# A windowed attention beside an S4 convolution: one stacked layout for Q and K, four loads an item, denominators turned on VectorE, wo prepared in steps, a new order of the attention's pieces

## The chip, the cores and the metric

One core of a Trainium2 chip runs the whole program. The metric is the device time in microseconds of one execution.

## The reference, cut to what is computed

```python
def _A_ref(x, wqkv, wo):            # x (1, 2048, 576), 32 heads of 18
    B, S, D = x.shape
    H = 32; Dh = D // H; W = 256
    qkv = (x @ wqkv).reshape(B, S, 3, H, Dh).transpose(2, 0, 3, 1, 4)
    q, k, v = qkv[0], qkv[1], qkv[2]
    scores = jnp.einsum("bhqd,bhkd->bhqk", q, k) * (Dh ** -0.5)
    mask = (idx[:, None] - idx[None, :] >= 0) & (idx[:, None] - idx[None, :] < W)
    p = softmax(jnp.where(mask[None, None], scores, -1e9), axis=-1)
    o = jnp.einsum("bhqk,bhkd->bhqd", p, v)
    return o.transpose(0, 2, 1, 3).reshape(B, S, D) @ wo

def _B_ref(u, A_re, A_im, B_re, B_im, C_re, C_im, log_dt, Dskip):   # u (1, 2048, 576), 128 states
    dt = jnp.exp(log_dt)[:, None]
    P = jnp.exp((dt * A)[:, :, None] * l[None, None, :])
    K = jnp.einsum("dn,dnl,dn->dl", Cc, P, dt * Bc).real
    y = causal_convolution(u, K)    # by FFTs of 4096 points
    return y + u * Dskip[None, None, :]

return jnp.concatenate([a, b], axis=-1)
```

## The kernel before

The program has three stages. In the first, `proj` multiplies x by wqkv (each f32 operand split in two f16 parts, 14 matmuls a tile, `mm14`), beside `tables`, which computes the S4 kernel K from outer products and sines, and `s1_u`, the first step of the convolution's transform of u. A planner gives their instructions an order on each engine. For each of four chunks of 512 rows, `proj` makes nine tiles of 128 channels of Q and K, each as a high and a low f16 part in st (pool pst, two buffers), and SP stores them: Q in qq (part, chunk, channel, row), K in kk (with the last 256 rows of the chunk before in front) and, for chunk 0, in k0. V goes to vd with a column of ones behind each head's 18 columns. The second stage, `s1_k`, is the first transform of the S4 kernel, stored in gk.

In the third stage the order is written out by hand (`manual_schedule`): each engine, and SP's queue with it, runs its instructions as the program issues them. There are 16 items: four chunks of 512 queries times four groups of eight heads. An item has five steps. In each step the loop in `build` advances generators: `att` (two tiles of scores with their exponentials, then the product with V of the step before, into po), `smax` (16 tiles of scores an item, each reduced by DVE to a row maximum, running 20 steps ahead; the maxima go as row 54 into Q, so that the next scores have them subtracted), `conv` (the convolution's spectra, products and inverse, then the last transform from hp), `norm` of the items before, and `wo` (the output projection). All tiles of scores, spectra and projections go through one PSUM ring of three slots (`slot`).

`load(i + 2)` stands in the second step of item i and fills one of three sets: f16 scores take stacked rows, for Q low, high, high and for K high, low, high of the 18 channels of a head (54 rows of each half of 64). It makes nine DMAs: for each half of Q one of 18 rows and one of 36 rows, the latter read twice over,

```python
nc.sync.dma_start(dv[64 * h + 18:64 * h + 54], src[0:1].to_broadcast([2, 18, 4 * n]))
```

for each half of K one of 36 and one of 18 rows, and V. Rows 54 up to 64 of K hold -32768, set by six memsets of POOL.

`norm` divides by the sums of the exponentials, which are rows 18, 50, 82 and 114 of osb (po copied by ACT). Four DMAs bring them to den (128 x 32), DVE takes the reciprocal, one DMA writes it to rd in DRAM, four read it back over 32 partitions each (rb), POOL multiplies, ACT and POOL split the result into two f16 parts, and four DMAs store it in od. `wo` loads od again for a finished chunk (oh, ol) and multiplies.

`wo_load` prepares wo once, at the end of item 0: four times load a quarter, take its absolute value on ACT and its maximum on DVE; then a power of two as scale; then four times load it again and split it in woh and wol. Its tile "raw" has one buffer.

Of the kernel before, what the change touches and what calls it, by code (L numbers as in the profile page):

```python
# [21 lines left out]
CQ = 512  # L22
CK = 768
# [80 lines left out]
class Kernel:  # L104
# [51 lines left out]
    def proj(self):  # L156
        nc, a, wp, dp, sp = self.nc, self.a, self.p["wq"], self.p["dram"], self.p["const"]
        self.qq = dp.tile([2, 4, D, CQ], F16, name="qq")
        self.kk = dp.tile([2, 4, D, CK], F16, name="kk")
        self.k0 = dp.tile([2, D, CQ], F16, name="k0")  # L160
# [33 lines left out]
        for c in range(4):  # L194
# [13 lines left out]
            for m in range(9):  # L208
                ps = self.p["pps"].tile([128, 512], F32, name="pp")
                self.mm14(ps, (wh, wl), (xh, xl), slice(m * 128, m * 128 + 128), slice(0, 512))  # L210
                st = self.p["pst"].tile([128, 2, 512], F16, name="qst")
                nc.scalar.activation(st[:, 0], ps, AF.Copy, scale=S)
                nc.vector.scalar_tensor_tensor(st[:, 1], ps, S, st[:, 0], op0=OP.mult, op1=OP.subtract)
                for z, off, f0 in ((self.qq, 0, 0), (self.kk, 256, D)):
                    r0, r1 = max(m * 128, f0), min(m * 128 + 128, f0 + D)
                    if r0 < r1:
                        s = st[r0 - m * 128:r1 - m * 128]
                        t = z[:, c, :, off:] if c or not off else self.k0
                        nc.sync.dma_start(t[:, r0 - f0:r1 - f0].rearrange("a p c -> p a c"), s)
                        if off and c < 3:  # L220
                            nc.sync.dma_start(z[:, c + 1, r0 - f0:r1 - f0, 0:256].rearrange("a p c -> p a c"),
                                              s[:, :, 256:])
                yield
# [254 lines left out]

    def slot(self):
# [43 lines left out]
    def inverse(self, t, ch, Y):  # L523
# [14 lines left out]
        if ch == 2:  # L538
            v = self.h.rearrange("(t s b c) a l j -> t s c (a l) b j", t=8, s=2, b=2)
            for s in range(2):  # L540
                for c in range(2):
                    nc.sync.dma_start(v[t, s, c ^ s], self.ho[64 * c:64 * c + 64, s])  # L542

    def conv(self):
# [20 lines left out]
        def load(m):  # L565
            hp[m] = fs.tile([128, 2, D], F32, name="hp")
            nc.sync.dma_start(hp[m].rearrange("p l j -> p (l j)"), hv[:, 2 * m * D:2 * m * D + 2 * D])

        load(0)
        for m in range(16):  # L570
            if m < 15:
                load(m + 1)
# [7 lines left out]
            for c in range(2):  # L580
                nc.sync.dma_start(ov[m, c][:, D:], y[64 * c:64 * c + 64].rearrange("p h j -> p (h j)"))
            yield

    def att_setup(self):
# [8 lines left out]
        for b in range(3):  # L593
            d = {"Q": ap.tile([128, 4, CQ], F16, name="Q%d" % b), "K": ap.tile([128, 4, CK], F16, name="K%d" % b)}
            for h in range(2):
                nc.gpsimd.memset(d["K"][64 * h + 32:64 * h + 64], -32768.0)
# [3 lines left out]
    def load(self, i):  # L600
        nc, (c, o), d = self.nc, divmod(i, 4), self.sets[i % 3]
        V = self.p["v"].tile([128, 12 * 76 + 16], F32, name="V")
        for nm, z, seq in (("Q", self.qq, (1, 0, 0)), ("K", self.kk, (0, 1, 0))):
            n = CQ if nm == "Q" or c == 0 else CK
            if n == CQ and nm == "K":
                z = self.k0
                d["k"], d["kc"] = d["K"].rearrange("p t n -> p (t n)")[:, :4 * CQ].rearrange("p (t n) -> p t n", t=4), 256
            elif nm == "K":
                d["k"], d["kc"] = d["K"], 0
            dv = d[nm].rearrange("p t n -> p (t n)")[:, :4 * n]  # L610
            for h in range(2):
                src = z[:, c, 144 * o + 72 * h:144 * o + 72 * h + 72] if z is not self.k0 else z[:, 144 * o + 72 * h:144 * o + 72 * h + 72]
                src = src.rearrange("a (i p) n -> a i (p n)", p=4)
                if nm == "Q":
                    nc.sync.dma_start(dv[64 * h:64 * h + 18], src[1])
                    nc.sync.dma_start(dv[64 * h + 18:64 * h + 54], src[0:1].to_broadcast([2, 18, 4 * n]))
                else:
                    nc.sync.dma_start(dv[64 * h:64 * h + 36], src)  # L618
                    nc.sync.dma_start(dv[64 * h + 36:64 * h + 54], src[0])
        nc.gpsimd.memset(V[:, 912:], 0.0)  # L620
        kc = d["kc"]
        t0 = 8 * c - 4 + kc // 64
        nc.sync.dma_start(V[:, kc // 64 * 76:912], self.vd[o, :, :, t0:8 * c + 8].rearrange("r k t e -> (r k) (t e)"))
        d["V"] = V

    def smax(self, i):
# [3 lines left out]
        for qb in range(8):  # L630
# [4 lines left out]
            for pp in range(2):  # L635
                ps = self.slot()
                for b in range(2):
                    for r in range(2):
# [3 lines left out]
                                         d["k"][rr, 2 * b + pp, k0 - d["kc"]:k1 - d["kc"]], start=True, stop=False, skip_group_check=True)  # L642
# [19 lines left out]
        for b in range(2):  # L662
            src = m16[16 * b:16 * b + 16].rearrange("s (h x) -> h s x", h=2)
            for r in range(2):
                nc.sync.dma_start(q[r:r + 1, 1024 * b:1024 * b + 1024].rearrange("o (s x) -> o s x", x=64), src[r ^ b])
# [30 lines left out]
    def att(self, i):  # L696
        nc, (c, o), d = self.nc, divmod(i, 4), self.sets[i % 3]
        po = self.p["po"].tile([128, 2, 512], F32, name="po")
        first = set()

        def pv(P, bl):
            for rel, o, q0, w in bl:
                kb = rel + 4
                for p in range(4):
                    for z in range(2):
                        nc.tensor.matmul(po[32 * p:32 * p + 32, z, q0:q0 + w],  # L706
                                         d["V"][64 * z:64 * z + 64, kb * 76 + 19 * p:kb * 76 + 19 * p + 32],
# [245 lines left out]
```

## Time and profile before

| | us |
|---|---|
| median of three runs (1357.79 to 1373.87) | 1358.03 |
| the profiled execution | 1366.19 |
| its span, from the first to the last instruction | 1364.4 |

| engine | busy in the span | share | instructions |
|---|---|---|---|
| PE | 844.7 us | 62% | 16426 |
| VectorE (DVE) | 554.0 us | 41% | 780 |
| ScalarE (ACT) | 573.4 us | 42% | 797 |
| GpSimd (POOL) | 287.8 us | 21% | 184 |

The mean granted clock of TensorE is 0.807 of full speed. The queue of SP carries 149.56 MB of the 155.96 MB that are moved. The shares are means over three stages; what bounds each is read from the windows and the waits below. In the rows, "A <- B" after a wait names what the engine waited for, as far as the profile shows it, and SPq is SP's queue of DMA issues.

### The profile page before, as it was taken

What the parts mean: (1) busy time and instruction counts of PE and PEld (TensorE: products, weight loads), DVE (VectorE), ACT (ScalarE), POOL (GpSimd) and SP (SyncE); (2) the same over time, 40 slices, a digit from 0 to 9 for tenths busy, and PEclk for the clock granted to TensorE, in tenths of its full rate; (3) what the DMA queues carried; (4) which work ended last, traced back from release to release, by engine and by line L of the source; (5) the groups of instructions that cost most, each with busy time, mean ns of one, the idle gap of its engine ahead of it and who ended that gap; (6) DMA issues with size and microseconds to landing.
All of it is one profiled execution on the core that took longest, in us unless ns stands there. A gap on an engine that the chain in (4) does not pass through costs nothing. (4 is left out here: it accounts for less than half of the span.)

```text
span 1364.4 us, 36796 instructions
## 1 busy us (share of the span) xinstructions
PE 844.7 (62%) x16426; PEld 500.2 (37%) x16426; DVE 554.0 (41%) x780; ACT 573.4 (42%) x797; POOL 287.8 (21%) x184
## 2 busy tenths in 40 slices
PE   1518898798888955703645465774467565267734
PEld 0204464464455543402322233442244343134413
DVE  3687667856565113413423332342333343132200
ACT  1857887577783221313321332432233243123521
POOL 0033443444342040100211121121021021011110
PEclk9999999988888965757866877976778887578977
DMA  9451242132222363522424343342525232354442
GB/s 271 143 175 64 81 105 88 53 76 90 68 78 67 112 215 148 189 69 67 139 63 117 126 116 120 87 139 77 163 79 175 73 102 61 106 173 135 132 146 87
DMA packets 108223, 155.96 MB, mean 114 GB/s; under 512 B 33745, under 2 KB 71697, under 8 KB 107873
## 3 DMA queue, kind: packets, MB, share of 16 engines
q1 hardware_dynamic: 106528, 149.56, 36.2%
q10 hardware_dynamic: 1504, 3.99, 1.1%
q8 instruction: 129, 2.11, 0.7%
q14 instruction: 30, 0.24, 0.1%
q0 software_dynamic: 32, 0.07, 0.0%
HBM read 94.26 MB, written 58.92 MB: 112 GB/s over the span
## 5 line engine op out<-in xcount | busy, mean ns | idle before, releaser
L654 DVE TENSOR_REDUCE m<-ring 128x2 f32<-128x640 f32 (+4 forms) x256 | 194.1, 780 | 407.2 <-PE ring L649 377.1
L641 PE MATMUL ring<-K,Q 54*64 54x320 f16 (+4 forms) x1024 | 94.1, 350 | 255.3 <-DMA K<-kk 132.7
L739 ACT ACTIVATE P<-ring,esc 128x1024 f32<-128x1024 f32 (+2 forms) x160 | 160.7, 1058 | 88.3 <-PE ring L735 88.3
L364 POOL TENSOR_TENSOR m<-A,tr 128x1024 f32<-128x1024 f32 x72 | 149.5, 2096 | 197.6 <-PE kp L402 165.2
L641 PEld LDWEIGHTS <-Q 54*64 54x64 f16 x1024 | 46.3, 117 | 302.2 <-issue 297.7
L519 POOL TENSOR_TENSOR Y<-t,t 128x384 f32<-128x384 f32 x24 | 24.0, 998 | 500.2 <-DVE t L517 430.2
L512 ACT ACTIVATE X<-ring 128x768 f32<-128x768 f32 x24 | 19.4, 810 | 220.2 <-PE ring L506 220.2
L402 PE MATMUL kp<-Q,m 128*32 128x64 f32 x4608 | 87.9, 229 | 30.3 <-DVE xp L137 10.8
L706 PE MATMUL po<-P,V 64*32 64x320 f32 (+4 forms) x2816 | 101.2, 409 | 0.6 <-issue 0.3
L402 PEld LDWEIGHTS kp<-Q,m 128*32 128x32 f32 x4608 | 74.8, 115 | 59.3 <-issue 36.8
L450 PE MATMUL pp<-ut,wu 64*128 64x288 f32 x128 | 48.0, 602 | 44.1 <-DMA ut<-in_u_dram 18.7
L726 PE MATMUL ring<-Q,K 55*64 55x320 f16 (+4 forms) x1408 | 68.8, 293 | 7.7 <-ACT P L739 2.6
L765 POOL TENSOR_TENSOR osb<-osb,rb 128x1024 f32<-128x1024 f32 x16 | 37.7, 2355 | 140.3 <-DMA Q<-m 84.5
L649 PE MATMUL ring<-sm,idb 64*64 64x128 bf16 x896 | 62.1, 244 | 0.0
L706 PEld LDWEIGHTS po<-P,V 64*32 64x32 f32 x2816 | 45.5, 123 | 39.2 <-issue 30.0
L154 PE MATMUL ring<-woh,oh 128*128 128x288 f16 x160 | 32.3, 334 | 41.9 <-DMA oh<-od 41.0
L154 PEld LDWEIGHTS <-oh 128*128 128x128 f16 x320 | 32.7, 111 | 65.4 <-DMA oh<-od 44.6
L576 PE MATMUL ring<-hp,i 128*64 128x288 f32 x128 | 24.8, 518 | 45.5 <-DMA hp<-h 43.5
L154 PE MATMUL pp<-xh,wh 128*128 128x512 f16 x180 | 48.6, 393 | 2.3 <-DVE xh L205 1.9
L536 ACT ACTIVATE ho<-ring 128x768 f32<-128x768 f32 x24 | 19.4, 810 | 72.5 <-PE ring L533 62.6
L154 PE MATMUL pp<-xh,wl 128*128 128x512 f16 x180 | 48.0, 391 | 0.0
L154 PEld LDWEIGHTS <-wh 128*128 128x128 f16 x324 | 31.5, 100 | 43.3 <-issue 11.0
(146 smaller groups left out, 1607.3 us busy)
## 6 DMA issues: line engine op xcount, KB each, us to landing
gx<-g SPq DMA_DIRECT2D x32, 288.0 KB
gk<-g SPq DMA_DIRECT2D x16, 576.0 KB
tx<-gx SPq DMA_DIRECT2D x8, 1152.0 KB
tk<-gk SPq DMA_DIRECT2D x8, 1152.0 KB
h<-ho SPq DMA_DIRECT2D x32, 288.0 KB
hp<-h SPq DMA_DIRECT2D x16, 576.0 KB
raw<-in_xT_dram SPq DMA_DIRECT2D x16, 512.0 KB
rb<-rd SPq DMA_DIRECT2D x64, 128.0 KB
```

Of the source, the lines that this page charges most:

```text
L154: self.nc.tensor.matmul(ps, u, v, start=(i == 0), stop=(i == len(ops) - 1))
L364: self.nc.gpsimd.tensor_tensor(m, A[:, ch, a0:a0 + 8].unsqueeze(3).to_broadcast(sh), tr[:, ch, part, 0:8].unsqueeze(2).to_broadcast(sh), o ...
L402: nc.tensor.matmul(kp[32 * st:32 * st + 32, c % 2 * JJ2 + j, :], m[:, ch, a0:a0 + 32], Q[:, ch, term % 2, :], start=(term == 0), stop=(ter ...
L450: nc.tensor.matmul(ps[r], self.wu[64 * r:64 * r + 64], ut[64 * r:64 * r + 64, 288 * k:288 * k + 288], start=True, stop=True)
L576: nc.tensor.matmul(ps[64 * c:64 * c + 64, hf, :288], self.i2, hp[m][:, c, 288 * hf:288 * hf + 288], start=True, stop=True, skip_group_chec ...
L641: nc.tensor.matmul(ps[z:z + 64, b, :n], d["Q"][rr, 2 * b + pp, 64 * qb:64 * qb + 64], d["k"][rr, 2 * b + pp, k0 - d["kc"]:k1 - d["kc"]], s ...
L649: nc.tensor.matmul(out, self.idb[rr], self.sm[rr], start=False, stop=True, skip_group_check=True)
L654: nc.vector.tensor_reduce(mv[:, :, 8 * pp + qb], ps[:, :, :n], axis=AX.X, op=OP.max)
L706: nc.tensor.matmul(po[32 * p:32 * p + 32, z, q0:q0 + w], d["V"][64 * z:64 * z + 64, kb * 76 + 19 * p:kb * 76 + 19 * p + 32], P[p % 2][64 * ...
L726: nc.tensor.matmul(ps[z:z + 64, b, off:off + w], d["k"][rr, 2 * b + pp, kc:kc + 64], d["Q"][rr, 2 * b + pp, q0:q0 + w], start=(k == 0), st ...
L739: nc.scalar.activation(P[pp][:, :, lo:hi], ps[:, :, lo:hi], AF.Exp, scale=self.esc)
L765: nc.gpsimd.tensor_tensor(osb, osb, rb, op=OP.mult)
```

## The change

1. Layout: Q and K are stored as the scores read them, qz and kz (chunk, half, 64 rows, 4 heads, 512 columns): the high part twice, the low part once, and rows 54 to 63 filled with -32768 from a tile of ones. A tile of st now takes two stores for each piece of a group of 72 channels.
2. `load` makes four DMAs of 128 rows (three for chunk 0): Q, K, the last 256 columns of K of the chunk before, V. V becomes part of the set.
3. `norm`: DVE transposes osb in blocks of 32 x 32, takes the reciprocal of column 18 of each block and transposes it, broadcast, back. The stores in od move one step later.
4. `wo_load` becomes a generator, advanced once a step from the start; "raw" has two buffers and is loaded two steps ahead; the maximum takes absolute values itself.
5. The order of a step: `att` runs across items and gives its pieces singly (a tile of scores, half of the product with V), with a tile of the maxima after every first or third piece; so the last product of an item falls in the next item's first step.
6. SP's issues of h, y, ya and the row of maxima are put off by `defer` to the next `flush` or the one after, at the start of a step. The last transform loads hp two tiles ahead (three buffers), `wo` waits one step more between its loads and its products.

```diff
+        self.qz = dp.tile([4, 8, 64, 4, CQ], F16, name="qz")
+        self.kz = dp.tile([4, 8, 64, 4, CQ], F16, name="kz")
+        ones = wp.tile([128, 4 * CQ], F16, name="ones")
+        nc.gpsimd.memset(ones, -32768.0)
+        for z in (self.qz, self.kz):
+            nc.sync.dma_start(z[:, :, 54:64].rearrange("c g r p n -> (c g) r (p n)"),
+                              ones[0:32].unsqueeze(1).to_broadcast([32, 10, 4 * CQ]))
...
+                for z, lo, f0 in ((self.qz, 0, 0), (self.kz, 1, D)):
+                    zz = z.rearrange("c g r p n -> c g (r p) n")
+                    for g in range(8):
+                        r0, r1 = max(m * 128, f0 + 72 * g), min(m * 128 + 128, f0 + 72 * g + 72)
+                        if r0 < r1:
+                            d = zz[c, g, 0:216].rearrange("(a j) n -> j a n", a=3)[r0 - f0 - 72 * g:r1 - f0 - 72 * g]
+                            t = st[r0 - m * 128:r1 - m * 128]
+                            nc.sync.dma_start(d[:, 1 - lo:3:1 + lo],
+                                              t[:, 0:1].to_broadcast([r1 - r0, 2, CQ]))
+                            nc.sync.dma_start(d[:, lo], t[:, 1])
...
+    def defer(self, fn, n=1):
+        self.later.append([n, fn])
+
+    def flush(self):
+        for x in list(self.later):
+            x[0] -= 1
+            if x[0] < 0:
+                self.later.remove(x)
+                x[1]()
...
+        self.flush()
+        self.flush()
         load(0)
+        load(1)
+        yield
         for m in range(16):
-            if m < 15:
-                load(m + 1)
+            if m < 14:
+                load(m + 2)
...
+        q, k = (z.rearrange("c (o h) r p n -> c o (h r) p n", h=2) for z in (self.qz, self.kz))
+        nc.sync.dma_start(d["Q"], q[c, o])
+        nc.sync.dma_start(d["K"][:, :, 256:], k[c, o])
+        if c:
+            nc.sync.dma_start(d["K"][:, :, 0:256], k[c - 1, o, :, :, 256:])
+        t0 = 0 if c else 4
+        nc.sync.dma_start(d["V"][:, t0 * 76:912], self.vd[o, :, :, 8 * c - 4 + t0:8 * c + 8].rearrange("r k t e -> (r k) (t e)"))
...
+    def att(self):
         pend = None
+        for i in range(16):
+            c, d = i // 4, self.sets[i % 3]
+            for n in (2, 4, 0, 1, 3):
+                bl = self.blocks(n, c)
+                P = []
+                for pp in range(2):
+                    P.append(self.scores(bl, d, pp))
+                    yield
+                    if pend is not None:
+                        self.pv(pp, *pend)
+                    yield
+                pend = P, bl, i, n == 3
...
+    def norm(self, i, osb):
+        nc, np_, (c, o) = self.nc, self.p["n"], divmod(i, 4)
+        T = np_.tile([128, 32, 32], F32, name="T")
+        nc.vector.transpose(T.rearrange("p k r -> p (k r)"), osb.rearrange("p z c -> p (z c)"))
+        R = np_.tile([128, 32], F32, name="R")
+        nc.vector.reciprocal(R, T[:, :, 18])
+        rb = np_.tile([128, 2, 512], F32, name="T")
+        nc.vector.transpose(rb.rearrange("p z (k r) -> p (z k) r", r=32), R.unsqueeze(2).to_broadcast([128, 32, 32]))
         yield
         nc.gpsimd.tensor_tensor(osb, osb, rb, op=OP.mult)
...
+        get(0)
         for c in range(4):
+            get(c + 1)
+            yield
+            yield
+            x = t.pop(c)
+            nc.vector.tensor_reduce(amx[:, c:c + 1], x, axis=AX.XY, op=OP.max, apply_absolute_value=True)
...
+                for k in range(81):
+                    i, s = divmod(k, 5)
+                    self.flush()
+                    step(at)
+                    step(sm)
+                    step(at)
+                    step(at)
+                    step(sm)
+                    step(at)
+                    step(sm)
+                    if (4 * k + 4) // 5 > (4 * k) // 5:
+                        step(conv)
...
+                    step(wo if i >= 5 else wol)
+                    if s == 1 and i < 14:
+                        self.load(i + 2)
```

`pv(half, ...)` computes the wide block of a step's product for half 0 and the other blocks for half 1, and copies po to osb after an item's last one.

## Rows read from the trace of the kernel before

**Rows 1.** Windows: busy time of each engine by stage, clock, DMA share, GB/s.

```profile
107.00:475.00 368.00, 319.78 (x5634) 187.48 (x5634) 223.80 (x345) 248.77 (x429) 138.82 (x68) 0.93 0.28 81
475.00:533.00 58.00, 31.66 (x258) 22.07 (x257) 6.06 (x8) 15.04 (x25) 16.07 (x8) 0.64 0.57 204
...
549.00:1308.00 759.00, 424.33 (x9951) 254.47 (x9950) 244.94 (x331) 246.44 (x269) 110.27 (x91) 0.75 0.39 115
```

**Rows 2.** Waits of PE over the span: us in total, times, longest.

```profile
PE ring L641 <- DMA K<-kk: 132.7, 20, 15.3
...
PE ring L641 <- DVE m L654: 47.2, 5, 45.7
...
PE ring L576 <- DMA hp<-h: 43.5, 6, 27.5
...
PE ring L154 <- DMA oh<-od: 41.0, 11, 24.7
...
PE ring L641 <- DMA K<-k: 12.7, 3, 7.9
```

**Rows 3.** Timeline at wo_load: start, duration, instruction, idle time before.

```profile
583.25 0.80 ACT L785 ACTIVATE raw<-raw 128x720 f32<-128x720 f32 x1 [5.86 <-DMA raw<-in_wo_dram]
```

**Rows 4.** Timeline of SP's queue: an item's load, and h's stores later.

```profile
918.31 0.36 SPq L759 DMA_DIRECT2D rd<-den  x1
...
922.32 0.60 SPq L618 DMA_DIRECT2D K<-kk  x1
...
1099.22 3.39 SPq L542 DMA_DIRECT2D h<-ho  x4
```

**Rows 5.** The chain that ended last, in order of time: start, duration, piece.

```profile
922.96 17.21 DMA K<-kk
...
963.18 11.09 DMA tk<-gk
...
1166.52 16.50 DMA hp<-h
...
1353.49 3.95 DMA out_dram<-ya
```

**Rows 6.** Windows of 5 us, columns as in rows 1.

```profile
965.00:970.00 5.00, 4.43 (x124) 2.74 (x128) 3.04 (x4) 2.82 (x3) 0.54 (x2) 1.00 1.03 388
...
995.00:1000.00 5.00, 4.31 (x96) 2.54 (x92) 2.79 (x5) 2.12 (x2) 3.67 (x3) 0.50 0.02 3
```

**Rows 7.** Timeline of ACT: the exponentials of a step, two in each row.

```profile
956.12 2.12 ACT L739 ACTIVATE P<-ring,esc 128x1024 f32<-128x1024 f32 x2 [0.86 <-PE ring L735]
...
961.88 2.12 ACT L739 ACTIVATE P<-ring,esc 128x1024 f32<-128x1024 f32 x2 [0.41 <-PE ring L735]
...
967.20 2.11 ACT L739 ACTIVATE P<-ring,esc 128x1024 f32<-128x1024 f32 x2
...
995.00 2.12 ACT L739 ACTIVATE P<-ring,esc 128x1024 f32<-128x1024 f32 x2 [1.21 <-PE ring L735]
...
1004.00 2.12 ACT L739 ACTIVATE P<-ring,esc 128x1024 f32<-128x1024 f32 x2
...
1057.84 2.12 ACT L739 ACTIVATE P<-ring,esc 128x1024 f32<-128x1024 f32 x2 [4.07 <-PE ring L735]
...
1065.84 2.11 ACT L739 ACTIVATE P<-ring,esc 128x1024 f32<-128x1024 f32 x2
...
1072.56 2.12 ACT L739 ACTIVATE P<-ring,esc 128x1024 f32<-128x1024 f32 x2 [1.83 <-PE ring L735]
```

**Rows 8.** Waits of SP's queue: us in total, times, longest.

```profile
SPq L219 <- DVE qst L213: 164.6, 34, 8.8
```

**Rows 9.** Groups by line: shape, count, busy us, mean ns, idle before.

```profile
L144 DVE TENSOR_REDUCE amx<-raw 128x1 f32<-128x1280 f32 x8 | 11.7, 1477 | 0.4 <-DMA raw<-in_xT_dram 0.4
```

**Rows 10.** Timeline at the end: osb of the last item, its product with rb.

```profile
1314.94 1.02 ACT L747 ACTIVATE osb<-po 128x1024 f32<-128x1024 f32 x1
...
1328.80 2.34 POOL L765 TENSOR_TENSOR osb<-osb,rb 128x1024 f32<-128x1024 f32 x1 [11.64 <-DMA rb<-rd]
```

More of the change, by code (lines that the diff above doesn't have):

```diff
@@ L593, in att_setup @@
         for b in range(3):
[L594 to L596 removed]
+            d = {"Q": ap.tile([128, 4, CQ], F16, name="Q%d" % b), "K": ap.tile([128, 4, CK], F16, name="K%d" % b),
+                 "V": ap.tile([128, 12 * 76 + 16], F32, name="V%d" % b)}
+            nc.gpsimd.memset(d["V"][:, 912:], 0.0)
             self.sets.append(d)
@@ L751, in norm @@
[L751 to L763 removed]
+    def att(self):
+        pend = None
+        for i in range(16):
[10 more added lines that the diff above has]
+                pend = P, bl, i, n == 3
+        for pp in range(2):
+            self.pv(pp, *pend)
+        yield
@@ new lines, in pv @@
+    def pv(self, half, P, bl, i, last):
+        nc, V = self.nc, self.sets[i % 3]["V"]
+        if self.po_of != i:
+            self.po_of, self.po, self.first = i, self.p["po"].tile([128, 2, 512], F32, name="po"), set()
+        po, first = self.po, self.first
+        wide = max(bl, key=lambda x: x[3])
+        for rel, o, q0, w in bl if half == 2 else [x for x in bl if (x is wide) != half]:
+            kb = rel + 4
+            for p in range(4):
+                for z in range(2):
+                    nc.tensor.matmul(po[32 * p:32 * p + 32, z, q0:q0 + w],
+                                     V[64 * z:64 * z + 64, kb * 76 + 19 * p:kb * 76 + 19 * p + 32],
+                                     P[p % 2][64 * z:64 * z + 64, p // 2, o:o + w], start=(p, z) not in first,
+                                     stop=False, skip_group_check=True)
+                    first.add((p, z))
+        if half and last:
+            osb = self.p["o"].tile([128, 2, 512], F32, name="osb")
+            nc.scalar.activation(osb, po, AF.Copy)
+            self.norms.append(self.norm(i, osb))
@@ L869, in build @@
                 self.att_setup()
-                self.osb, self.done = {}, -1
+                self.norms, self.later, self.done, self.po_of = [], [], -1, -1
                 self.load(0)
@@ L915 @@
+                while self.norms or conv or wo:
+                    self.flush()
+                    for g in list(self.norms):
+                        if next(g, 0) == 0:
+                            self.norms.remove(g)
+                    if conv and next(conv, 0) == 0:
+                        conv = None
+                    if wo and next(wo, 0) == 0:
+                        wo = None
+                while self.later:
+                    self.flush()
 def kernel(**inputs):
```

203 lines of the change are left out of this document (59 added, 144 removed).

## The prediction

> **What bounds the kernel now.** I first cut the span by stage and read each engine's busy time there [rows 1]. Up to 475 us (projections beside the S4 tables) PE is busy 320 of 368 us: PE-bound, at a granted clock of 0.93. From 475 to 533 us (the S4 kernel's first transform) the DMA engines carry the stage, 204 GB/s with PE half idle. From 549 to 1308 us (attention beside the long convolution) no engine is busy for more than 424 of 759 us, so this stretch is made of waits. I then read the waits of PE, which works in order, so that each stops everything behind it [rows 2]. The maxima's matmuls (line 641) wait 132.7 us for K from kk and 12.7 us for K from k0; one wait of 45.7 us stands as "DVE m"; the last transform waits 43.5 us for hp; the output projection 41.0 us for od, 24.7 of it at the very end. That makes 275 us, all but those 24.7 inside the loop or at its rim.
>
> Next, why each is so long. The 45.7 us is `wo_load`: ACT stands behind the first of eight loads of wo [rows 3], each load waits for the pass before because "raw" has one buffer, and the queued exponentials and DVE's maxima wait behind. K is late for two reasons. On SP the item's nine loads stand behind `rd<-den`, which waits for DVE's reciprocal, which waits for the four loads of den: it goes out at 918.31 and the last big K piece (216 KB) at 922.32 [rows 4], when PE is about to need K. That piece then takes 17.2 us [rows 5], though the DMA engines can move 388 GB/s in a good 5 us [rows 6]. The first transfer of hp has a like 16.5 us in the chain [rows 5].
>
> Last, I read the steps of the loop from the starts of the exponentials (two a step) [rows 7]. With the clock at 1.00 a step takes 5.76 and 5.32 us (956.12 to 967.20). The step after a K wait (995.00 to 1004.00) takes 9.0 us, with the clock at 0.50, TensorE's 1.2 GHz level, though PE is busy for over 4 of 5 us [rows 6]. A step with a half tile of the output projection takes 8.0 and 6.7 us [rows 7].
>
> **The change, part by part**, against the profiled execution (1366.2 us; the median of the runs is 8.2 us less).
>
> Projections: 55 stores of st become 192 (24 pieces of a head group a chunk, two stores each, four chunks). At about half a microsecond an issue that is 70 us more of SP over 368 us. SP stood 164.6 us of the stage waiting for st to be made [rows 8], and a store that is issued later only holds one of two st buffers longer: 0, at worst +10 us if SP falls behind. The stores carry a quarter more bytes, in a stage where the DMA share is 0.28 [rows 1]: nothing. The rows of ones add 2.6 MB at the start, before the first projections; hidden they cost 0, moved alone at the 204 GB/s of [rows 1] 13 us; I take +3, since they overlap DVE's passes over x.
>
> First transform, 475 to 533 us: the loads of items 0 and 1 fall from eighteen to six. They share the engines with gk's stores, which the stage waits for; their bytes grow by 0.3 MB. From -12 (the stage at 260 GB/s) to +3; I take -5. The six memsets of K leave POOL, which nobody waited for.
>
> wo: one step loads a piece, two steps later it is reduced, and all 17 steps fit into the first four items, two buffers deep. Its ACT and DVE work (under 2 us a piece) stays in the loop. One reduction over partitions holds DVE for about a microsecond. -45 us.
>
> Loads: four of 128 rows, 1.8 MB. There is no den, rd or rb ahead of them on SP, and the output stores, h and the row of maxima are issued a step or two after they are made, so that SP seldom stands. Q and K can go once item i-1's scores are through, V after its last product, so the lead is two to three steps, 11 to 16 us. The transfer: 1.8 MB at 388 GB/s is 4.6 us; at the 204 GB/s of the first transform 8.7 us; with four issues and the landing 8 to 12 us. So most waits go. What is late next is a load behind the convolution's tx and tk (2.3 MB, 11.1 us to land from tk's issue [rows 5]), issued just ahead of it in three items of sixteen: about 3 us each. From -145 to -85 us; I take -135.
>
> The Trainium skill (DMA: Bandwidth & Descriptors, Why a DMA increments its semaphore by 16 and not by 1) says that a transfer runs on the largest number of engines up to 16 that divides the outermost dimension of both sides. By it the old K piece, 36 rows from a source whose outer dimension is 2, ran on two engines, and 128 rows run on sixteen, so that no K wait would be left and the sum would be 10 us lower; the 17.2 us for 216 KB [rows 5] agree with it.
>
> hp: two tiles ahead instead of one, and the first load a convolution step before its use. The first wait of 27.5 us [rows 2] keeps the time for h's last stores, their landing and a load, some 11 us, less one step: 5 us left, -22; of the other five waits, 16 us, 12 go: -34. od: one step more between its loads and the product; of the 16.3 us in the loop -12.
>
> Clock: every wait of 10 us or more is followed by about two steps at the lower level. The step at 995.00 took 9.0 us, its like at the full clock 5.3 to 5.8 us: 6 to 7 us a wait for the two steps, 12 such waits: -78 if all recover. But the clock also dips behind short waits, and some will stay: I take -40, from -20 to -70.
>
> Denominators: two transposes of 1024 columns and a reciprocal an item on DVE in place of nine small DMAs and a DRAM round trip. No transpose is in the trace. Its nearest row is DVE's pass over 1280 columns, 1.48 us [rows 9], so 1.2 us; at half that speed 2.4 us. Three instructions in a row hold the maxima behind them, and with a ring of three PSUM slots PE feels most of it: +2 us an item. Against it, the new order puts two score tiles and maxima between an item's last product and the next item's first, where PE used to wait for ACT's copy of po, about 2 us. Net 0, from -15 to +35. The new order (tile, maximum, half of V, and so on) gives ACT and DVE turns; I count nothing for it, from -25 to +20.
>
> End: from osb (1314.94) to its product with 1/den (1328.80) lie 13.9 us [rows 10], 1.0 of it the copy; three DVE instructions take 2.7 in place of 12.8. The last half of V follows its exponentials directly. -15 us.
>
> Sum: +3 +0 -5 -45 -135 -34 -12 -40 +0 -15 = -283: 1083 us for a profiled execution, 1075 for the median. A check by steps: 80 steps of 5.1 us (five an item, the one after osb shorter) and 24 half tiles at 2 us more [rows 7] make 456; with 28 us of waits left, 484; the sum leaves 759 - 266 = 493 us for the loop.
>
> **Rivals.** *Loads still late.* The lead shrinks with the steps: at 5 us a step it is 10 us where SP reaches the load only in its own step. If tx and tk, h's stores and od's loads stand ahead of it in most items, each waits 5 us, and the clock stays low behind it: K keeps 70 us and half of the clock's 40 is lost, 1075 + 60 + 20 = 1155 us. For it: a tk load took 11.1 us [rows 5]. Against: the DMA share of the loop is 0.39 [rows 1]. The Trainium skill (DMA: Bandwidth & Descriptors, Queues, rings and completion order) says that descriptors are consumed in ring order on each engine; with 128 rows on all of them every load would queue behind tx and tk, as this rival has it.
>
> *The ring decides.* With three slots in turn, scores and spectra evacuated by ACT, maxima by DVE, the transposes in DVE's way and POOL's product ahead of Y, the step falls to about 6 us and no further, 0.9 us over the 5.1: 80 x 0.9 = +72, 1147 us. For it: DVE's 245 us of the loop [rows 1] and 16 x 2.8 us more are 290 us, 3.6 of 5 us in each step. Against: with the clock at 1.00 PE was busy 4.4 of 5 us [rows 6].
>
> *Slower: stores of the projections in a row.* qz and kz are written by interleaved pieces and the ones beneath. If a store had to wait until the one before in its tensor has landed, each would cost its issue, 0.6 us, and up to 3.95 us as a store of the output [rows 5]: 192 x 4.55 = 874 us of SP, with some 130 other issues 939, in a stage of 368 us: +571, 1646 us. It decides from a landing of about 2.5 us, where the stage grows by the 283 us gained. Against it: h's four stores, interleaved in the same way, go out within 3.4 us together [rows 4].
>
> *Nothing of the sort:* if the deferred issues reach SP in the old order, only wo, the norm and the end are gained; that is -45, 0 and -15, 1298 us, at 0.03 with all else that leaves little.
>
> **How the numbers follow.** Forecast 0.64, loads late 0.15, ring 0.16, slower 0.02, and 0.03 for little gain. The unknown costs alone reach from 1003 to 1220; the range of 1010 to 1180 us takes in both middle rivals. A measurement tells about 2% from no change. Faster by more: 0.96 (the first three and most of the last); within: 0.02; slower: 0.02.
>
> **What would show it.** Right: no wait of PE over 10 us after 550 us; waits for K under 30 us in all; no idle stretch at wo; exponentials 5 to 5.5 us apart without the output projection; a clock of 0.85 or more in the loop; osb to product under 6 us; the stage up to 475 us within 10 us. Wrong: waits for K over 60 us, a transpose over 2 us, SP busy without a break in the projections, or PE's waits for "ACT P" and "DVE m" growing past 150 us.

## The result and the profile after

The kernel after takes 1100.37 us (median of four runs, 1098.81 to 1109.06) against 1362.69 us before (median of four; the table ahead of the prediction has the first three of them): a ratio of 0.8079, interval 0.8008 to 0.8149. The profiled execution took 1100.82 us, its span is 1099.0 us and its mean granted clock 0.886, against 0.807.

I read the same views again. First the windows of the kernel after by stage (PE, PEld, DVE, ACT, POOL busy; clock; DMA share; GB/s):

```profile
107.00:475.00 368.00, 306.22 (x5377) 178.30 (x5374) 231.50 (x344) 245.36 (x412) 132.00 (x65) 0.89 0.35 98
475.00:533.00 58.00, 42.33 (x372) 31.84 (x372) 6.89 (x10) 19.23 (x36) 0.20 (x3) 0.82 0.67 233
549.00:1056.00 507.00, 397.36 (x9883) 229.97 (x9878) 281.75 (x361) 248.11 (x263) 114.24 (x79) 0.89 0.51 161
```

The loop, from the first exponential to the last step's, is 506 us long (550.0 to 1056.4), before 757 (549.4 to 1306.3, nearly the third window of [rows 1]). PE works for 397 us of its window, at a clock of 0.89: what was made of waits is now PE at work for most of its length. The waits of PE in the kernel after, total, times and longest, answer to [rows 2]:

```profile
PE ring L154 <- DMA oh<-od: 16.5, 4, 13.4
...
PE ring L645 <- DVE m L658: 16.5, 15, 1.8
...
PE ring L730 <- DMA Q<-m: 11.0, 6, 5.5
PE ring L548 <- DVE m L658: 10.7, 2, 10.3
...
PE ring L645 <- DMA K<-kz: 9.8, 3, 6.7
...
PE ring L595 <- DMA hp<-h: 4.5, 1, 4.5
```

K fell from 145.4 us to 9.8, hp from 43.5 to 4.5, od from 41.0 to 16.5, of which 13.4 is the end. Of the 45.7 us at wo a wait of 10.3 is left. The wait for m (the row of maxima on its way into Q) has grown from 2.1 to 11.0 us, and a wait of up to 1.8 us for a maximum, once an item, is new. The longest wait for K that is left I put down to SP's queue just ahead of it; no run takes these transfers away. First the queue, then that piece in the chain that ended last (its issue, and us to its landing):

```profile
720.06 0.39 SPq L830 DMA_DIRECT2D oh<-od  x1
...
724.94 3.38 SPq L557 DMA_DIRECT2D h<-ho  x4
...
731.29 0.50 SPq L506 DMA_DIRECT2D tk<-gk  x1
731.83 0.50 SPq L623 DMA_DIRECT2D Q<-qz  x1
...
733.05 0.92 SPq L626 DMA_DIRECT2D K<-kz  x1
```

```profile
733.05 12.12 DMA K<-kz
```

Behind od's eight loads, h's stores and tx and tk, K takes 12.1 us to land, and PE stands 6.7 us for it.

At the end the copy to osb is followed by its product in 4.2 us, where [rows 10] had 13.9; ACT's rows first, then POOL's:

```profile
1060.07 1.02 ACT L763 ACTIVATE osb<-po 128x1024 f32<-128x1024 f32 x1 [0.43 <-PE po L756]
...
1064.26 2.34 POOL L775 TENSOR_TENSOR osb<-osb,T 128x1024 f32<-128x1024 f32 x1 [8.85 <-DVE T L773]
```

From the last step's exponentials to the end of the span it is 40 us, before 56.

Two things moved that I had not seen coming. The first product of the projections starts at 146.28 us, before at 107.39, and their last at 489.84, before at 474.45. The next stage gave that back: the first transform takes 38 us (491 to 529), before 52, so that the first exponential comes at 550.0, before at 549.4.

### The profile page after: what moved, and what is told of

Its sections match the earlier page's. It is cut to its first block, busy times and chain, and to the rows that moved or that the text cites. A ratio compares the mean times of both kernels' runs of the same rounds, so it can differ in the third digit from the quotient of the medians.

```text
span 1099.0 us, 36700 instructions
## 1 busy us (share of the span) xinstructions
PE 819.5 (75%) x16426; PEld 480.1 (44%) x16426; DVE 604.8 (55%) x812; ACT 582.6 (53%) x797; POOL 272.4 (25%) x166
## 4 chain that ended last, share of the span: by engine, by line
PE 42%; DVE 19%; DMA 14%; ACT 14%; issue 5%; SPq 3%; POOL 2%; POOLq 0%; DVEq 0%; ACTq 0%
PE pp L154 11%; ACT P L743 6%; PE ring L154 5%; PE kp L407 4%; PE ring L521 3%; DVE m L658 3%; DMA gk<-g 3%; PE po L756 3%; PE ring L548 3%; PE pp L455 3%; PE ring L730 3%; DMA K<-kz 3%; PE ring L645 2%; PE x L303 2%; DMA ut<-in_u_dram 2%
## 5 line engine op out<-in xcount | busy, mean ns | idle before, releaser
L743 ACT ACTIVATE P<-ring,esc 128x1024 f32<-128x1024 f32 (+2 forms) x160 | 168.1, 1060 | 79.3 <-PE ring L739 77.5
L645 PE MATMUL ring<-K,Q 54*64 54x320 f16 (+4 forms) x1024 | 87.0, 328 | 52.4 <-DVE m L658 16.5
L756 PE MATMUL po<-P,V 64*32 64x320 f32 (+4 forms) x2816 | 106.8, 378 | 3.9 <-ACT osb L763 3.6
L730 PE MATMUL ring<-Q,K 55*64 55x320 f16 (+4 forms) x1408 | 70.8, 281 | 21.3 <-DMA Q<-m 11.0
L730 PEld LDWEIGHTS <-K 55*64 55x64 f16 x1408 | 30.8, 110 | 87.8 <-issue 75.2
L217 DVE SCALAR_TENSOR_TENSOR qst<-pp,qst 128x512 f16<-128x512 f32 x36 | 24.7, 687 | 59.5 <-ACT qst L216 52.0
L653 PE MATMUL ring<-sm,idb 64*64 64x128 bf16 x896 | 56.9, 230 | 0.0
L775 POOL TENSOR_TENSOR osb<-osb,T 128x1024 f32<-128x1024 f32 x16 | 37.7, 2354 | 74.9 <-DVE T L773 54.2
L315 ACT ACTIVATE ab<-k 128x512 f32<-128x512 f32 (+1 forms) x54 | 31.8, 589 | 37.7 <-DVE k L314 37.6
L548 PE MATMUL ring<-Y,i 32*64 32x192 f32 x768 | 40.8, 351 | 13.4 <-DVE m L658 10.7
L455 PEld LDWEIGHTS pp<-ut,wu 64*128 64x128 f32 x128 | 19.6, 243 | 63.9 <-issue 25.1
```

The source lines that it names most:

```text
L455: nc.tensor.matmul(ps[r], self.wu[64 * r:64 * r + 64], ut[64 * r:64 * r + 64, 288 * k:288 * k + 288], start=True, stop=True)
L548: nc.tensor.matmul(ps[64 * (b % 2):64 * (b % 2) + 64, b // 2, 192 * s:192 * s + 192], i1[32 * b:32 * b + 32, o:o + 64], Y[32 * b:32 * b + ...
L645: nc.tensor.matmul(ps[z:z + 64, b, :n], d["Q"][rr, 2 * b + pp, 64 * qb:64 * qb + 64], d["K"][rr, 2 * b + pp, k0:k1], start=True, stop=Fals ...
L653: nc.tensor.matmul(out, self.idb[rr], self.sm[rr], start=False, stop=True, skip_group_check=True)
L730: nc.tensor.matmul(ps[z:z + 64, b, off:off + w], d["K"][rr, 2 * b + pp, kc:kc + 64], d["Q"][rr, 2 * b + pp, q0:q0 + w], start=(k == 0), st ...
L743: nc.scalar.activation(P[:, :, lo:hi], ps[:, :, lo:hi], AF.Exp, scale=self.esc)
```

## The experiments

Each kernel is the one after with the edit whose main lines are shown. Times are medians, ratios are to the kernel before, differences to the 1100.37 us of the kernel after; "in the loop" means from the first exponential to the last. The kernel after did not run beside these, and its own interval (0.8008 to 0.8149) is nearly 10 us wide to either side: a difference under 10 us is not settled by the medians alone.

**Why K was late.** Theory: the nine pieces are slow by themselves. Rival: they only stood behind the denominators' chain on SP. Three kernels: each cause put back alone, then both.

```
-        nc.sync.dma_start(d["Q"], q[c, o])
-        nc.sync.dma_start(d["K"][:, :, 256:], k[c, o])
...
+                    nc.sync.dma_start(dv[64 * h:64 * h + 36], src)
+                    nc.sync.dma_start(dv[64 * h + 36:64 * h + 54], src[0])
```

> The changed kernel with the old layout of Q and K and the nine loads of an item; all else as changed, V in the set. Theory 1 (the old K pieces are slow by themselves, whatever stands before them on SP): a piece takes about 17 us against a lead of 12 to 15 us, so K waits come back, 5 to 8 us in each of 14 items, with the clock behind them: waits for K of 70 to 110 us, 1100 + 60 to 130 us. Theory 2 (the loads were late only because SP reached them late): waits for K stay under 30 us, within 20 us of 1100.

Old layout, nine loads an item: 1194.85 us, ratio 0.8777 (0.8750 to 0.8804), 94.5 us more than the kernel after. The first exponential is where it was (550.2 us), so the loop has the loss. The waits for K, and a big piece in the chain, issue to landing:

```profile
PE ring L655 <- DMA K<-kk: 77.0, 16, 13.9
...
PE ring L655 <- DMA K<-k: 14.8, 3, 8.3
```

```profile
771.10 15.46 DMA K<-kk
```

```
-        nc.vector.transpose(T.rearrange("p k r -> p (k r)"), osb.rearrange("p z c -> p (z c)"))
...
+            nc.sync.dma_start(den[32 * p:32 * p + 32], osb[32 * p + 18:32 * p + 19].rearrange("o r c -> o (r c)"))
...
+        nc.sync.dma_start(rd.rearrange("p (k c) -> (p k) c", c=32), den)
```

> The changed kernel with the denominators by way of den, rd and rb in DRAM, nine small DMAs an item, the load of an item again behind rd on SP. Theory 1 (128 rows land in 8 to 12 us, so the lead is enough even behind rd): waits for K under 40 us, the end longer by 10 us, 1100 + 10 to 40 us. Theory 2 (SP's chain was what made K late): waits for K over 100 us, 1100 + 100 us or more. Rival on the other side: without the transposes in DVE's way, faster by up to 25 us.

Denominators through DRAM: 1179.40 us, ratio 0.8669 (0.8627 to 0.8710), 79 us more. The waits for K, then SP's queue and the chain at one item:

```profile
PE ring L645 <- DMA K<-kz: 67.3, 11, 17.9
```

```profile
711.21 2.46 SPq L770 DMA_DIRECT2D den<-osb  x4
...
718.74 0.35 SPq L774 DMA_DIRECT2D rd<-den  x1
719.14 0.42 SPq L623 DMA_DIRECT2D Q<-qz  x1
719.61 0.60 SPq L624 DMA_DIRECT2D K<-kz  x1
720.25 0.63 SPq L626 DMA_DIRECT2D K<-kz  x1
```

```profile
720.25 7.12 DMA K<-kz
```

The same picture as in [rows 4]: the loads leave right behind `rd<-den`. The new piece of K (256 KB) lands in 7.1 us, the old one (216 KB) in 15.5, and yet PE waits 67.3 us in all: the loads leave when it is about to ask for them.

Both together (the edits of the two, no other):

> Changed: both the old layout with its nine loads an item and the denominators by way of DRAM together, the rest as in the kernel after. One alone cost 94.5 us (nine loads) and 79 us (denominators by DRAM). If they are two causes that add up: 1260 to 1290 us, waits of K and Q at 150 to 190 us. If both act through one thing, the lateness of the same transfers, of which the later one decides: 1195 to 1220 us, waits of 90 to 120 us. If they make each other worse (slow loads that also start late): over 1300 us.

1342.80 us, ratio 0.9831 (0.9802 to 0.9860).

```profile
PE ring L655 <- DMA K<-kk: 214.8, 24, 24.2
```

In waits for K: 9.8 us with neither, 91.8 and 67.3 with one, 230.5 with both (15.7 of them for k0). In time: 94.5 + 79.0 = 173.5 us singly, 242.4 together. Put back together they cost more than the sum. I read it so: a lead of some steps takes up most of a late start or of a slow transfer; together they use it up, and all that follows is wait. No run varies the lead. Seen from the kernel with both, taking one away gains 163 us (the nine loads) or 148 us (the round trip through DRAM), and taking the second away as well adds 79 or 95. Neither theory alone was right. With the pair put back, the rest of the change (wo, hp, od, the order, the deferred issues) is left with 20 of the 262 us.

**Deferred issues.**

```
     def defer(self, fn, n=1):
-        self.later.append([n, fn])
+        fn()
```

> Changed: every issue that the kernel put off by a step or two (the stores of the halves of ho, of the output, of the maxima) is made at once again; the rest is as in the kernel after (1100 us). Theory: with the transposes SP still has these stores, and each of them waits for its data at the head of SP's queue with the next item's loads behind it; the waits of K and Q grow from 21 us to 40 to 60 us and the time to 1120 to 1140 us. Rival: what held SP was the denominators' chain alone, two issues of which waited for each other; the stores' data are nearly ready when SP comes to them, the waits stay under 30 us and the time within 10 us of the kernel after.

1101.85 us, ratio 0.8064 (0.8023 to 0.8104): no change. The waits for K in the whole span are 18.7 us instead of 9.8, those for m 2.3 instead of 11.0. The rival held: what held SP was the denominators' round trip; the deferral only moves some us from one wait to another.

**hp one tile ahead.**

```
-        load(1)
-        yield
...
-            if m < 14:
-                load(m + 2)
+            if m < 15:
+                load(m + 1)
```

> Changed: the loads of hp stand one tile ahead again, the first directly ahead of its use, as before the change; the rest is as in the kernel after (1100 us). Theory: the waits for hp come back at 35 to 45 us and the time is 1122 to 1140 us. Rival: the waits were long because SP stood with the old loads in front of h's stores and hp; without those the first wait is the landing alone, 10 to 15 us, the others under 10 us in all, and the time is at most 1115 us.

1108.26 us, ratio 0.8127 (0.8108 to 0.8147): 8 us more; the intervals overlap, but in the traces PE waits 7.1 us more in the loop. It waits 10.8 us for hp, 9.1 of it the first time. The rival held. Of the 39 us that these waits lost, 33 stay lost with one tile ahead. That does not make them the queue's alone, for the kernel above with both old loads and old denominators, which loads hp two tiles ahead, has

```profile
PE ring L590 <- DMA hp<-h: 7.9, 2, 7.5
```

Either remedy by itself takes most of the wait for hp; what the second tile ahead adds to the first is 6 to 8 us.

**wo in one go.**

```
         for c in range(4):
-            get(c + 1)
-            yield
-            yield
...
+            nc.scalar.activation(t, t, AF.Abs)
+            nc.vector.tensor_reduce(amx[:, c:c + 1], t, axis=AX.XY, op=OP.max)
...
                     step(wo if i >= 5 else wol)
+                    if k == 4:
+                        self.wo_load()
```

> The changed kernel with wo prepared in one go after item 0, raw with one buffer. My theory: the wait of 45.7 us comes back for the 10.3 us that the steps still show, plus two slow steps: +35 to +50 us. Rival (its loads now find free DMA engines and the stall shrinks, or other waits hide in it): +20 us or less.

1120.85 us, ratio 0.8235 (0.8206 to 0.8264): 20.5 us more, though one wait is long (among the waits of the whole span):

```profile
PE ring L645 <- ACT P L743: 51.3, 22, 38.1
```

PE stands 38.1 us, from 578.98 on, and about half of it is not paid: the wait of 10.3 us that the kernel after has at the reduction is gone, and that for m falls from 8.7 us in the loop to 0.8; what is late elsewhere lands meanwhile. The rival held. A stall is worth its length less the waits that it covers.

**The wait of 10.3 us that wo leaves.** In the kernel after, DVE stands 9.5 us for one reduction over partitions on POOL; POOL's rows at that place, then DVE's, then PE's:

```profile
609.71 1.00 POOL L534 TENSOR_TENSOR Y<-t,t 128x384 f32<-128x384 f32 x1 [9.61 <-PE ring L739]
610.66 1.00 POOL L535 TENSOR_TENSOR Y<-t,t 128x384 f32<-128x384 f32 x1
611.62 2.12 POOL L780 TENSOR_TENSOR oh<-osb,oh 128x1024 f16<-128x1024 f32 x1
619.64 0.38 POOL L135 PARTITION_ALL_REDUCE og<-om  x1 [5.91 <-issue]
```

```profile
620.05 0.15 DVE L136 TENSOR_SCALAR og<-og 128x1 f32<-128x1 f32 x1 [9.51 <-POOL og L135]
```

```profile
621.20 1.23 PE L548 MATMUL ring<-Y,i 32*64 32x192 f32 x12 [10.26 <-DVE m L658]
```

The reduction takes 0.38 us, but comes 5.9 us after POOL is done with its products, while it waits for nothing that the profile shows.

```
-        po, self.so = self.pow2_scale(amx, "o")
...
+        nc.gpsimd.partition_all_reduce(g, m, 128, bass.bass_isa.ReduceOp.max)
+        yield
+        yield
+        nc.vector.tensor_scalar(g, g, 1e-30, None, op0=OP.max)
...
```

> Changed: the sum over the partitions of wo's maxima is issued two steps ahead of the first of its readers on VectorE, not directly ahead of it. The arithmetic is the same. Theory: the wait of TensorE of 10.26 us at 610.94 is VectorE standing 9.5 us in front of that sum; VectorE works on meanwhile and the wait falls under 3 us, the time by 5 to 10 us, to 1090 to 1095 us. Rival: GpSimd itself is held for the 6 us ahead of the sum, and what GpSimd owes to others (the products and the conversions) comes late in VectorE's place: the wait moves and the time stays within 3 us of the kernel after.

1091.26 us, ratio 0.7996 (0.7969 to 0.8023): 9 us less. The interval overlaps a little with that of the kernel after (from 0.8008), but all six runs lie under its lowest, and the wait itself is gone from the trace. POOL idles as before, but nobody waits behind it:

```profile
616.76 2.12 POOL L780 TENSOR_TENSOR oh<-osb,oh 128x1024 f16<-128x1024 f32 x1
624.83 0.38 POOL L811 PARTITION_ALL_REDUCE og<-om  x1 [5.95 <-DVE T L769]
```

The theory held. The order of the change itself had kept 10 of wo's 45 us.

**The order of a step.**

```
-                    if pend is not None:
-                        self.pv(pp, *pend)
-                    yield
+                if pend is not None:
+                    self.pv(0, *pend)
+                    self.pv(1, *pend)
+                yield
...
-                    step(at)
+                    step(at, 2)
                     step(sm)
                     step(at)
-                    step(at)
-                    step(sm)
-                    step(at)
-                    step(sm)
+                    step(sm, 2)
```

> The changed kernel with the old order in a step: two tiles of scores, a maximum, the whole product with V, two maxima. My prediction counted nothing for the new order: within 15 us of 1100. Rival (the alternation is what fills the ring): PE's waits for ACT P and DVE m grow by 30 us or more, +25 to +60 us.

1096.35 us, ratio 0.8058 (0.8036 to 0.8081): 4 us less, which the intervals do not tell from none. The loop in the windows:

```profile
549.00:1051.00 502.00, 380.82 (x9915) 237.74 (x9918) 279.90 (x361) 241.59 (x264) 114.12 (x79) 0.90 0.51 163
```

PE waits 87.4 us there for ACT's P and DVE's m (with the alternation 67.1), but is busy for 380.8 us instead of 397.4, with as many instructions (9915 and 9883). Alternating takes 20 us of these waits away (12 of all waits) and comes with 17 us more in the products. Not all of the 17 need be the order's: the clock was 0.90 here and 0.89 in the kernel after, and the kernel with few loads below, which alternates too, has 385 us at 0.93. The prediction's count of nothing held, and the rival, by which the old order would cost 25 us or more, fell.

**The price of the transposes.** Each issued three times:

```
         nc.vector.transpose(T.rearrange("p k r -> p (k r)"), osb.rearrange("p z c -> p (z c)"))
+        nc.vector.transpose(T.rearrange("p k r -> p (k r)"), osb.rearrange("p z c -> p (z c)"))
+        nc.vector.transpose(T.rearrange("p k r -> p (k r)"), osb.rearrange("p z c -> p (z c)"))
```

> Changed: each of the two transposes of an item is issued three times, 64 further instructions of VectorE of 1.25 us, 5.0 us an item, 80 us in all. Theory (the prediction's net 0): VectorE has room, and TensorE feels only the last item's 5 us at the end and some us in the ring: 1105 to 1120 us. Rival (the prediction's upper bound): three instructions in a row hold the maxima and TensorE feels half or more of them: 1140 to 1180 us, and the waits named DVE m grow by 30 us or more.

1180.58 us, ratio 0.8663 (0.8629 to 0.8696): 80 us more for 80 us of DVE. The first of PE's waits by size:

```profile
PE ring L521 <- DVE m L658: 57.1, 10, 6.6
```

The theory fell, and the rival held in its way (its bound of 1180 us is met to a microsecond): the waits named "DVE m" grow by 59 us in the loop, from 41.6 to 101. DVE is busy for 282 of 507 us in the loop of the kernel after, and yet has no room at this place. The transposes hold the maxima, these hold their PSUM slots, and PE stands up to 6.6 us. That 80 us cost 80 is partly chance. In the two traces, 85 us apart, all of PE's waits in the loop grow by 61 us, the products take 17 us more at a lower clock, and the end takes 7 more. The loop's window, to set beside that of the kernel after:

```profile
549.00:1135.00 586.00, 415.51 (x9907) 236.94 (x9906) 356.02 (x421) 249.17 (x264) 114.12 (x79) 0.84 0.45 141
```

The kernel after shows the same at a smaller size, DVE's rows and PE's at one item:

```profile
795.99 1.25 DVE L769 STREAM_TRANSPOSE T<-osb 128x1024 f32<-128x1024 f32 x1
797.27 0.35 DVE L771 RECIPROCAL R<-T 128x32 f32<-128x32 f32 x1
797.65 1.25 DVE L773 STREAM_TRANSPOSE T<-R 128x1024 f32<-128x1024 f32 x1
798.82 2.25 DVE L658 TENSOR_REDUCE m<-ring 128x2 f32<-128x640 f32 x3
```

```profile
799.66 0.33 PE L645 MATMUL ring<-K,Q 54*64 54x320 f16 x4 [1.82 <-DVE m L658]
```

PE waits 1.82 us behind the second transpose. In the loop "DVE m" comes to 41.6 us in the kernel after and to 25.0 with the denominators through DRAM: by this pair the transposes cost 16.6 us of waits, about 1 us an item. The two kernels with nine loads agree: the same wait of the maxima's products for DVE is 16.8 us with the transposes and 2.0 with the denominators through DRAM.

**The start.**

```
-        ones = wp.tile([128, 4 * CQ], F16, name="ones")
...
         S = 2.0 ** -24
+        ones = wp.tile([128, 4 * CQ], F16, name="ones")
```

> Changed: the fill of the ones and its two transfers stand just before the loop of the projections, not ahead of the loads of the scales. Theory: those two transfers drew the loads of the maxima of x back (VectorE's maxima at 107 to 131 us, before the change at 70 to 96), and with them the first product from 107.4 to 146.3 us; they go back, the last product of the projections comes at 475 instead of 490 us and the first exponential at 535 to 545 instead of 550 us, total 1085 to 1095 us. Rival: the second stage has its own bound (in the kernel before it took 52 us from 475.7, in the one after 38 us from 491, both to 528 us), so the first exponential stays at 548 to 551 us and the time within 3 us.

1087.72 us, ratio 0.7971 (0.7947 to 0.7994): 12.7 us less. The first product comes at 135.93 us, the last at 474.80, the first exponential at 535.98. The theory's times held, not its way: the first maximum of x is at 70.8 again, the last still at 127.3, nearly as in the kernel after (130.8; before, 95.7). In SP's queue the two transfers moved less than in the program, from 66.40 and 66.77 us to

```profile
68.59 0.53 SPq L195 DMA_DIRECT2D qz<-ones  x1
...
78.48 0.59 SPq L195 DMA_DIRECT2D kz<-ones  x1
```

and so they still stand among the loads of x. Of the 10 us by which the first product comes sooner, 3 lie ahead of the reduction over partitions of x's maxima and 8 in it: it starts 0.14 us behind its input, in the kernel after 8.37 us. The stage gained 15 us at its last product; which wait gave them back is not shown. The first transform keeps its 38 us, so the rival fell.

**What the loads still cost.**

```
     def load(self, i):
...
+        if i > 2:
+            return
```

> Changed: Q, K and V are loaded for the first three items alone, and the other thirteen compute with these data, so the output is not the reference's; every product, exponential and store stays. Theory: what is left of a step (5.7 us without the output projection) is TensorE and the ring of score tiles, and the loads cost only the 21 us of waits for K and Q and a little of the clock: 1070 to 1085 us, steps still 5.5 to 5.7 us. Rival: the loads' 23 MB also hold back the convolution's loads, h and od, and their waits split the steps: under 1065 us, steps at 5.2 us.

1087.31 us, ratio 0.7976 (0.7959 to 0.7994). The loop is shorter by 22 us (558.4 to 1042.7), the first exponential 8 us later; 6 of the 8 are there already at the last product of the projections, ahead of the loads. Its loop in the windows:

```profile
558.00:1043.00 485.00, 384.46 (x9887) 223.97 (x9886) 280.88 (x360) 248.09 (x264) 114.15 (x79) 0.93 0.39 123
```

PE is busy 12.4 us less at a higher clock, and the waits sum to 97.6 instead of 106.3 us. The eighth item takes 27.4 us, in the kernel after 29.6, the twelfth 30.0 and 28.6: 5.5 to 6 us a step. In the loop the theory's size held, with 12 us of it from the products and 9 from the waits; the total lies 2 us outside, by the later start. With loads that cost nothing the step would still not be at 5.1.

**All three gains together** (old order in a step, reduction ahead, late ones):

> Changed: the three edits that each made the kernel after quicker, together: the old order in a step (by itself 4 us), the sum over partitions of wo's maxima two steps ahead of its readers (9 us), the ones just before the loop of the projections (13 us). Theory: they act in three places, so that they add up: 1072 to 1080 us. Rival: the first two act in the same loop, where what one gives is taken by the next limit: 1082 to 1088 us, as with the late ones alone.

1077.66 us, ratio 0.7901 (0.7873 to 0.7929), clock 0.908: 22.7 us under the kernel after, where the three singly made 25.8. They nearly add up, as the theory had it.

## Why the prediction was right, and by what it was off

The measured 1100.4 us lies in the range, with the forecast 25 us low. 8 us of that are the step from the profile to the median: before, the profiled execution was 8.2 us above the median of three runs (3.5 above that of four); of the kernel after it was not. The other 17.7 us, by profile: the stages up to 550 us +2.6, the loop +15.5, the end -0.5. Point by point:

| term | counted | in the trace, PE's waits or busy time in the loop |
|---|---|---|
| K | -135 | 145.4 to 9.8: -135.6; new for m, +8.7 |
| hp | -34 | 39.9 to 4.5: -35.4 |
| wo | -45 | 45.7 to 10.3: -35.4 |
| od in the loop | -12 | 14.3 to 0.4: -13.9 |
| denominators | 0 | other "DVE m" 23.7 to 31.3: +7.6 |
| clock | -40 | busy 422.8 to 397.4: -25.4 |
| new order | 0 | "ACT P" 58.9 to 25.5: -33.4 |
| end | -15 | -15.5 |
| ones, projections, first transform | -2 | last projection +15.4, from there to the first exponential -14.8: +0.6 |

The rows are a reading of the trace and not what each part is worth by itself: with the two old causes of K put back, the kernel gains 20 us, where my terms for wo, hp and od alone had summed to 91. PE then waits 230.5 us for K, where before the change it waited 145.4: as the other waits go, those for K grow. The sum came out near because all of them went together.

*K.* The size of the waits was right, to the microsecond by luck, and the two causes that I named were both there. What I did not say, and only the pair of experiments shows, is that either alone would have left 67 to 92 us of waits; the rival "loads still late" has the size of these two kernels, though not their cause (tx, tk, h and od ahead of most loads). The Trainium skill (DMA: Bandwidth & Descriptors, Queues, rings and completion order) has descriptors consumed in ring order: the 12.1 us of K behind od's loads, tx and tk agree with it, and it costs 6.7 us at that place, not in most items. By its rule on the number of engines (same page, Why a DMA increments its semaphore by 16 and not by 1) no wait for K would have been left; 9.8 us were, with the piece itself down from 15.5 to 7.1 us, so the trace agrees with it in the direction; no view here shows which engines a piece ran on.

*hp, od.* Right in size. For hp the cause that I named, the second tile ahead, is one of two that each take most of the wait. For od no run takes the extra step away alone; with old loads and old denominators put back PE waits for it in the loop not at all, so that it was not the queue that went.

*wo.* Mis-sized: -35 by the waits and 20 by the experiment. "One reduction over partitions holds DVE for about a microsecond" is the step that failed; it held DVE for 9.5, because the reduction did not start until 9.1 us behind its input.

*Clock and order.* These two are to be read together. With the old order PE is busy 380.8 us, 42 less than before, near the -40 that I counted, but the way to it was wrong in two places, so that this is luck. I had 12 waits of 10 us or more; in the loop of the kernel before there are 12 over 5 us, 8 over 9 and only 5 that come to 10. And the two steps that I set against each other were not alike: the one of 5.76 us from 956.12 ran at a mean clock of 0.72 and not of 1.00, the one of 9.0 us from 995.00 at 0.71. The clock is not what parts them, and they hold different work (176 and 200 products). The net of 0 for the new order holds: 17 us more in the products, 20 less in two waits. Why the products get longer the runs do not show, and why ACT's P is waited for less even in the old order (36.6 us) I have not settled.

*Denominators.* The duration was right (1.25 us, counted as 1.2), the net of 0 was not: I gave them +2 us an item and set against it a gain at ACT's copy of po that no row showed. They cost some 16.6 us of waits, and PE now also waits for osb, 3.6 us in all.

*Steps.* The check by 5.1 us a step was too low: with 28.6 us for the twelfth item, a step takes 5.7, and 80 x 5.7 and the 48 us for half tiles make 504 of the loop's 506 us. The rival "the ring decides" had 6, and so two thirds of its 0.9 us a step came true. The kernel with few loads shows that the loads are not what keeps the step there. No run changes the ring of three slots, so whether it does stays open. The rival of slower stores fell: in the projections SP still stands 94.5 us waiting for st.

*Start.* The two terms were wrong, and their sum right by luck: +3 for the ones against +15 in the trace, -5 for the first transform against -14. The second lies a little beyond the bound that I had written (-12): from its first to its last product the stage moves 287 GB/s, before 211, with fewer and larger loads between gk's stores, and ACT waits 18.2 us for these, before 35.6. The layout, with the ones, stores and loads that belong to it, is the cause of both: with the old one put back the first product comes at 108.4 us and the first transform takes 51.7 us again. What the ones alone did to the first product is shown by the kernel with late ones for 10 of its 39 us (146.3 to 135.9), and there most of it by way of a reduction that starts sooner; the other 28, which that kernel still has without its last product coming late, I did not follow up.

Of what was to show it: waits for K under 30 us, the clock and osb to product came out; no wait over 10 us (there are two, 10.3 at wo's reduction and 13.4 for od at the end), the steps, and the stage up to 475 us did not.

## What to carry to other kernels

When a wait has two causes, slow and late, do not judge either from one experiment: here putting one back costs 95 or 79 us, both 242, and so taking one away from both gains 148 or 163. A queue that holds one round trip charges it to all that stands behind it, so price a wait at the queue's head and not at the transfer that PE happens to name. And an operation that is moved onto an engine with idle time is not free: look at what the next instruction of that engine holds (here a PSUM slot), for there 80 us of work brought 61 us of waits and cost 80 us in all.

## What the runs showed of the hardware that I had not expected

The reduction over partitions of wo's maxima on POOL (0.38 us) starts 5.7 to 6.2 us after POOL's last tensor operation in all twelve kernels where such an operation stands close ahead of it (5.91 us in the kernel after, 5.95 with the reduction ahead, 5.87 with the transposes tripled), and 9.0 to 9.4 us after its input. In most of them it waits for nothing that the profile shows. Where POOL had been idle for 8 us or more it started 0.14 us after its input: wo's in the kernel before and with wo in one go, x's with late ones. Why, no run shows. A transpose of 128 x 1024 f32 in blocks of 32 x 32 takes 1.25 us on DVE, 1.22 ns a column, where its maximum over 1280 columns takes 1.15 ns [rows 9]. And the same products, in as many instructions, take PE 381 or 397 us as they are grouped or alternated, at granted clocks of 0.90 and 0.89.
